# DeltaNet and token mixer on one core: odd head pairs of the last element with their two chunks exchanged

## The chip, the cores and the metric

The kernel runs on one core of a Trainium2 chip. The core has TensorE (PE, the matmuls; its weight loads are listed apart as PEld), VectorE (DVE), ScalarE (ACT), GpSimd (POOL) and SyncE (SP, which here issues every DMA). PE writes its results into PSUM, 8 banks of 2 KB on each of 128 partitions; DVE and ACT read them from there. The time is the device time of one execution in microseconds.

## The reference

Two blocks, one after the other, in float32. The first is DeltaNet over batch 4, 8 heads, 768 tokens, head size 48. Each head keeps a 48x48 state, and each token updates it:

```python
k_n = k / (np.linalg.norm(k, axis=-1, keepdims=True) + 1e-06)
for t in range(S):
    y[:, :, t] = np.einsum('bhd,bhde->bhe', q[:, :, t], state)
    v_old = np.einsum('bhde,bhd->bhe', state, kt)
    state = state + bt[:, :, :, None] * np.einsum('bhd,bhe->bhde', kt, vt - v_old)
```

Its output, seen as 4 x 768 x 384, is the input x of an MLP mixer: `u = x + (relu(x^T w_tok1) w_tok2)^T`, then `u + relu(u w_ch1) w_ch2`, with 256 token features and 1536 channel features.

## The kernel before

**Units and steps.** An element (b, one of the batch of 4) has 768 tokens, cut into 6 units of 128 tokens; units are numbered u = 0 to 23 over the whole batch, so element 3 is units 18 to 23. A unit has two chunks of 64 tokens, cc = 0 and 1. The recurrence goes chunk by chunk, t = 0 to 47, and t = 2u + cc; element 3 is steps 36 to 47.

**Layout.** The 8 heads are four pairs, p = 0 to 3, of two heads, i = 0 and 1. `PAR` names the two halves of the 128 partitions. Data by token (k, v, and what is made from them) are held "stacked": head i of pair p with chunk cc lies on partition half `i ^ cc`, at column slot (p, cc). So one chunk of the two heads of a pair fills both halves. `stacked` (L397) loads k or v so, with 4 DMAs, one per head parity and chunk, each of 4 pairs x 64 tokens. Data by feature (`kqts`, the transposed keys and queries, and the states `s_t`) hold head i on half i, in 48 of its 64 rows (`FEATS`).

**Preparation.** For each unit `load_kq` and `load_v` fetch, and `prep` (L430) computes: ACT squares the stacked keys (`ksq`, L440), DVE and ACT turn the sums into a scale, `cs` multiplies it with beta (L453), from unit 12 on DVE transposes keys and queries (L366, called at L469 and L488), PE multiplies keys with keys and queries (`p_g`, L502), and DVE masks the products into `gm` (L507). `gm` holds per (pair, chunk) three column blocks: `KC` (scaled keys, 48), `TC` (a 64x64 triangular matrix, inverted by DVE in `invert` by rounds of four units, L637 and L642, and joined by PE in `join`), and `GC` (masked query-key products, 64). `load_v` ends with POOL scaling v (L414).

**One step of the recurrence**, `recur(t)` (L740), with the state `s0` and the next state `s1`:

- `p_k` (L757): 8 products, keys times state, weights 48 rows x 64 columns. Head i reads its rows on half i and writes half `i ^ cc`. A 64x64 quarter of the array is given by the row half and the column half of a product; the 8 products of a step use two quarters.
- `rest` (L762), DVE: p_k - v.
- `p_y` (L775), queries times state, and `p_w` (L779), TC times rest, alternating.
- `w_t` (L783), ACT: copy of p_w.
- `p_s` (L791), the state's update, with 64 columns of gm, of which the first 48 are keys, and the second half of p_y (L792), alternating.
- `s1` (L801), DVE: s0 - p_s (a copy at the first step of an element, L803).
- y (L806), ACT: two copies of p_y, one per head parity, 64 partitions x 192 each, into the mixer's input `xb`.

A matmul in float32 shows as two records, so 8 products are 16 records. The first step of an element has no p_k and no first half of p_y; the last has no p_s.

**PSUM.** Four groups of tiles share the 8 banks, one bank each: "prep" 2, "seq" 2, "mlp" 3, and `p_warm` 1, the target of idle matmuls at the start (jobs x, z, Y). p_k, p_y, p_w and p_s each take a free bank of "seq" when they begin and give it back when they have been read.

**The mixer** (`mixer(b)`, L943) follows each element: token products (p_1 L950, p_h L963), transposes (p_ut L973, copied by ACT L977), channel products (p_r L922 by 15 sums of blocks, evacuated by ACT L931, DVE L934 and ACT L938; p_o L1052, added by DVE L981 and L1004). Its products are the bulk of PE's work, and it runs beside the recurrence of the next elements.

**Order.** The planner of the tile library is off. Every job is a Python generator, and the long string `order` (L1124) says which one advances next: `r37*2` advances recur(37) by two yields, `k20` load_kq(20), `p21` prep(21), `m2` mixer(2), `i5` the inversion of round 5, `v18` load_v(18), and so on. Each engine runs its instructions strictly in that order, and SP issues the DMAs in it; the semaphores are put in by the library.

`load_beta` (L238) makes `beta_st`, beta by token and head, with one product per chunk and parity that picks the heads with every second column of the identity (`p_b`, L247).

Of the kernel before, what the change touches and what calls it, by code (L numbers as in the profile page):

```python
# [13 lines left out]
C = 64  # L14
# [9 lines left out]
def kernel(  # L24
# [72 lines left out]

    def ps_seq(shape, name):
        return psum.tile(shape, FP32, name=name, tag="seq", bufs=2)
# [119 lines left out]
    p_warm = psum.tile([128, 4, 128], FP32, name="p_warm", tag="warm", bufs=1)  # L219

    def keep_warm(m):

        zero = warm[:, 0:128]
        while True:
            nc.tensor.matmul(
                p_warm[:, 0:m], zero, zero[:, None, :].to_broadcast([128, m, 128])
            )
            yield

    def warm_tiles():  # L230

        while True:
            for j in range(2):
                for r in PAR:
                    nc.tensor.matmul(p_warm[r, j], warm[r, 0:C], warm[r, 0:128])
            yield

    def load_beta():  # L238
# [6 lines left out]
        for c in range(NQ):  # L245
            for par in range(2):
                nc.tensor.matmul(  # L247
                    p_b[PAR[par ^ c % 2], c], rows[:, c * C : (c + 1) * C],
                    ident[: B * H, par : B * H : 2],
                )  # L250
# [146 lines left out]
    def stacked(dst, src, u):  # L397
        rows = heads_of(src, u)
        for par in range(2):
            for cc in range(2):  # L400
                nc.sync.dma_start(
                    out=dst[PAR[par ^ cc], :, cc], in_=rows[par, cc]
                )
                yield
# [25 lines left out]
    def prep(u):  # L430
# [3 lines left out]
        if u < TU:  # L434
            kp, qp = kpad[slot(u)], qpad[slot(u)]
        gm, kqt, nrm = gm_of(u), kqts[place(u)], nrms[place(u)]
        bet = beta_st[:, b, :, 2 * c : 2 * c + 2]
# [15 lines left out]
        nc.vector.tensor_tensor(  # L453
            out=cs, in0=ksum.rearrange("s (p c) -> s p c", c=2), in1=bet, op=ALU.mult
        )
# [41 lines left out]
        for p in range(NP):  # L497
            for cc in range(2):
                for i in range(2):
                    f = PAR[i] if u < TU else FEATS[i]  # L500
                    nc.tensor.matmul(  # L501
                        p_g[cc][PAR[i ^ cc], p], kqt[f, p, cc, 0], kqt[f, p, cc]  # L502
                    )
        yield
        for cc in range(2):
            assert cc == 0 or before_in(u) is None or before_in(u) in walked
# [233 lines left out]
    def recur(t):  # L740
# [10 lines left out]
        heads = [(p, i, PAR[i ^ cc], PAR[1 - i]) for p in range(NP) for i in range(2)]  # L751

        if c > 0:
            p_k = ps_seq([128, NP, D], "p_k")
            for p, i, r, _ in heads:
                f = FEATS[i]
                nc.tensor.matmul(p_k[r, p], kqt[f, p, cc, 0], s0[f, p])  # L757
# [4 lines left out]
            nc.vector.tensor_tensor(  # L762
                out=rest, in0=p_k, in1=vsts[u][:, :, cc], op=ALU.subtract
            )
            yield
        else:
            rest = vsts[u][:, :, cc]

        assert u in scaled and u in joined
        p_y = ps_seq([128, NP, D], "p_y")  # L770
        p_w = ps_seq([128, NP, D], "p_w")
        for p, i, r, o in heads:
            if c > 0:
                f = FEATS[i]
                nc.tensor.matmul(  # L775
                    p_y[o, p], kqt[f, p, cc, 1], s0[f, p],
                    start=(p == 0), stop=False,
                )
            nc.tensor.matmul(p_w[r, p], gm[r, 2 * p + cc, TC], rest[r, p])  # L779
# [7 lines left out]
        if on:  # L787
            p_s = ps_seq([128, NP, D], "p_s")
        for p, i, r, o in heads:
            if on:  # L790
                nc.tensor.matmul(p_s[PAR[i], p], gm[r, 2 * p + cc, 0:C], w_t[r, p])  # L791
            nc.tensor.matmul(  # L792
                p_y[o, p], gm[r, 2 * p + cc, GC], w_t[r, p],
                start=(c == 0 and p == 0), stop=(p == NP - 1),
            )
        if cc == 1:
            walked.add(u)
        yield
        if on:
            if c > 0:  # L800
                nc.vector.tensor_tensor(out=s1, in0=s0, in1=p_s, op=ALU.subtract)  # L801
            else:
                nc.vector.tensor_copy(out=s1, in_=p_s)  # L803
            yield
        for i in range(2):
            nc.scalar.mul(  # L806
                y[:, :, D * i : D * i + D], p_y[PAR[1 - i]], 1.0 if c else -1.0
# [319 lines left out]
    k4 p1 k5*2 k2*3 p2*2 v0*2 w3*3 p2 k3 p3 p2 p3 p2*4 k5 p2*2 p3 p4 w13 p1 w18 z w2 p0  # L1127
    p3*2 v0 p2 p3 v1 p2*2 p3*3 k5*2 k6 p2 p3 p4 k4 p3*3 p4 w13 w6 p2*2 p1*2 p3*2 k5 p4
    w13 k7*2 p3 i0*6 p5 i0*2 w6 p4*3 k6 p4 i0*4 k6 p4*2 i0*2 k6 i0 p4 w18 k6 z w18*2 i0
    p4*3 p5*2 v1 w13 Y h1*2 h0 i0 k7*2 p6*2 f0*2 w8 w17 f0 h2 h0*2 w8 f1 p5 k7 h0*2 p6  # L1130
    h0*2 h2 p5 v0 w17 f1*2 p7 w8*2 z k8 p4 w6*2 j0 f2 p5*3 k8 w17 f2 j0 h1 v0 j0 h1*3 z
    v1 h1 p7 j0*2 j1 f2 h2*2 w11 h2 z p5 x h2*2 p6 r0*2 p5 w17 r0 k8 w11 v1*2 w11 k8
    w11 r0 p5 p4 k7 w14*2 p5 k9 p5 w14 r0 k8 k9 p5 r1*2 j1 j2 j1 w14 k9*2 h3 f3 r1 p5
    r1 p5 i1 k6 h3 p6*2 Y w9*2 j1 r1 j2 r1 p6 r1 r2 z i1 f3 i1 w0 j1 k9 p8 r2 w0 r2*2
    v2 j2 f3 h3 k9 r2 x h3 p6 h3*2 i1*4 k10 h3 p6 r2*2 w9 p6 i1 r3*2 i1 p7 w0 p6*3 v2*3
    k10*2 w0 k10 p7 r3 v2 w5 r3*4 j3 j2*2 p8 r4*2 j3*2 r4 v3 w9 r4 p7 i1 p7 i1 p8 p7
    w24 i1 p7*2 r4 k8 r4 p8 j3 i1 r5 i1 r5 j3 r4 i1 k10 p7 w5 p7 w5*2 p7 v3 r5*2 p7 p9
    v3*3 w16 r5*3 r6 p6*2 w24 i1 v4 p8*2 v4 p8 w24*2 p6 r6 h5 i1 r6 h5 w27 w16 h4 r6 p7
    h4 p8*2 p6 w16 w27 w16 p7 r6 f4*3 v4 p8*2 r6 w28 p9 p8*2 r7 w27*2 v4*2 h4 p9 r6 p7
    r7 p9 p7 w26 h4*4 p9*3 r7 p9 r7 p9 r7*2 w26*3 p8 w7 p9*4 j4 f5 p8 f5*2 v5 Y p10  # L1140
    w28*2 j4 p10 m0 w7*3 j4*2 r8*2 r7 j4 h5*2 p8*2 h5 p9*4 h5 r8*2 w28 w29 r8 w29 j5
    w29 r8 i2 w15*2 r9 w15 k11 r8 k11 w29 w15 i2*2 v5 h5 j5 i2 m0 r9 i2*4 j5 v5 i2 r9
    i2*3 x j5 r9*3 j5 k11 w22 k11 v7 w22 v7 v5 p10 w4*2 v7 w12 i2 r10 i2*2 w12*2 v5 i2
    w4 m0 i2 r10 p10 w4 i2 m0 k10 k12 w12 r9 k12 v7 w19 i2 r10*5 k12 i2 m0 i2 r11*2 i2
    w19*2 w21 i2 p10 r11 w22 k11 w19 k12 i2 w22 k12*3 v6 w25 v6 r11*2 i2*2 v6 p10 r11
    w31 i2*2 v6 k12*3 v6 p10 i2 p10*2 i2 k12 p10 m0 p10 m0 i2*2 m0 w25 m0 k11 f6 p11*2
    f6*3 m0*2 w21 f7*4 p10 m0*3 f8 w27 p10 w25 m0 w31 k12 p12*2 w31 f8*2 j6 w31 p11 m0
    p11 w23 f8 j6*2 m0 p12 w21*2 w25 j7*3 w29*2 m0 f9*2 w32 p11 r12 j8 p11 p12 w20 p11
    r12 s m0 v7 r12 w25 r12 w23 p10*3 f9 r12 j8 r13 w23 p12 w23 j8 m0 p11 r13*3 p11*2
    w23 x w32 f9 v8 w30 w20 r13*2 k13 w32 w20 p10 r13 p11*3 w20 k13 r14*2 p12 k13 w32  # L1150
    p12 k13*3 m0*2 k13 w30 m0 k13 p11 w30*2 v8 k13 r14 k13*2 r14 p12*2 p11 k13 p12 p13
    r14 p12*3 m0 p12 p13 r14*2 m0 p13 w23 w25 p13 w33 v8*2 m0 j9 r15 p13 m0 w23 p13 r15
    w25 m0 p11 m0 r15 p13 r15 w33 m0*2 r15 p13*2 k14 w33 r15 k14 p13*2 w33 r16 m0 r15
    v8 k14*4 p12 w33 p11 r16 w27 w33 w31 m0 w27 w33 w29 w31*2 p13*2 j9 m0 p13*2 m0 j9
    k14 r16 j9 r16*3 k14 p14*2 r16 m0 r17*2 p14*3 m0*2 r17 i3 r17 i3*4 v10 m0 v10 r17*3
    i3*3 k15 m0 i3*2 v9 r18 i3*2 p14 m0 v10 k14 m0 i3 v9 i3 k15*4 v9 k15*3 m0*2 k14
    i3*9 k14 i3 k14 i3 p14 v9*2 m0*3 k15 r18 k15 p14 i3*6 m0*2 i3 v10 j9 k15 m0*4 k15
    m0*9 r18 p14*2 f11 r18*4 f10*2 p15*2 f12 v10 f12 f11 m0*2 p15*2 f10*2 f13 m0 r19
    p15 f12 f11 m0 f11 m0 r19 p14 f13 j10 f13 m0*2 r19 p15 j10 j11 r19*2 k16*8 m0*2 r19
    j10 j11 v11*3 r20 m0*2 r20 r19 j12 j11 r20 p15 k16 r20 m0 r20*2 p16*2 p15*3 k16 v11  # L1160
    p16*2 r21 r20 r21 m0 p15 r21 p16 r21 j12 p14 j12 k16*2 p14*2 k17*2 r21*3 m0 s k17*5
    p16*2 r22 v11 m0 r22*3 p16 m0 k17*4 r22 s v12 s j13 s p16 r22 k17 p16 r22 r23 p16*3
    v12 r23 v12 p15*4 p17*3 p14 p17 m0 p17 r23 m0 p17*2 r23 m0*2 p16 r23 p17*3 v12 p16
    m0 p17*4 m0 s m0 s*3 p17 m0 f12 m0 j13 s*4 r23 m0*3 v12 m0 i4*5 m0 i4*2 k18*8 m0 i4
    j13 r24 m0 i4 m0*2 r24 f13 r24 k18 m0 i4*2 k18 i4 m0*2 p18 i4 k18 p18*2 m0*2 i4 r24
    i4*3 m0 i4*2 k18 p18 r25 p18 m1 v14 r24 v14*3 i4 r25 m1*2 i4 k19 i4 k19*2 m1*3 r25
    k19 i4*2 v13 j13 r25 i4 p18 r25*2 i4 k19*4 m1 i4*2 m1 r25 v13*2 i4*2 v13 i4 j13 i4
    p19 r26 m1*2 p18 k19*4 m1 v13 r26 p19 m1*5 p18 f14 r26 f14 r26 p18 r26 f15 m1 r26
    m1*3 r26 m1*2 p19 f14 r27*2 f14 m1 r27 f15 p19 f15*2 p19 k20*5 p18 j14 m1*2 p18 p19
    r27*2 j14 j15 m1*2 j14 r27 m1 r27 k20*2 s j15 r28 p18 j15 p19 v14 k20*4 r28 m1*3  # L1170
    k20 m1 v15*2 s*2 p19 v15*2 r28*2 p19 r28 v15 m1 f16*3 r28 r29 p19 p20*2 r28 r29
    p20*2 p19 p20 k21*4 m1*3 p19 k21*4 r29*2 p20 p18*2 p20 m1*3 f17*2 m1*3 r29*3 j16
    m1*2 f17 m1 k21*4 m1*5 r30 j16 m1 r30 p20 m1 p19 m1 p18 m1 j16 p21 r30 p21 p20
    p19*2 p20 r30*3 p20 p21 p20 r31 p20*2 p21 r30 m1 r31*2 v16 r31 v16 m1 p21 f16 k22
# [55 lines left out]
```

## Time and profile before

| what | us |
|---|---|
| median of 3 runs | 647.36 (644.69 to 653.36) |
| the profiled execution | 649.33 |
| its span, first to last instruction | 647.5 |
| PE busy | 609.4 (94%) |
| DVE busy | 445.6 (69%) |
| ACT busy | 258.1 (40%) |
| POOL busy | 107.9 (17%) |
| L757 p_k, one record (mean) | 0.228 |
| L1052 p_o (weights wc, moving r), one record (mean) | 0.330 |
| L934, DVE addition of p_r, one (mean) | 0.684 |

The page of a profile gives busy time by engine, then 40 equal slices of the span with the busy share in tenths and PE's granted clock, the DMA queues, the chain of work that ended last, and groups of instructions by line. Durations of matmul records overlap: a record's duration is its latency, and what a group costs PE is the time from its first start to the next group's first start. A timeline row is start, duration, engine, line, operation, output<-inputs, shapes (output<-input, partitions x elements) and, in brackets, the engine's idle time before it and what ended that. "SPq" rows are DMA issues, and their duration is SP's time to issue them.

### The profile page before, as it was taken

Reading aid. Unit: us, or ns where it says so; the run is one execution under the profiler, and the core shown is the slowest. Engines: PE = TensorE matmul, PEld = TensorE weight load, DVE = VectorE, ACT = ScalarE, POOL = GpSimd, SP = SyncE. Lnnn points to the kernel's source line nnn. Section 1 sums busy time; section 2 is a strip of 40 time slices with the busy share of each in tenths; the row PEclk is TensorE's granted clock in tenths of the full one; section 3 lists DMA queues with packets and bytes.
Section 4 is the critical chain, followed back from the end, with each engine's and each line's share of the span. In section 5 each row is a group of like instructions: output and inputs, shape, how many; then the busy total and the mean of one; then the engine's idle time right before and its main releaser. Section 6 shows DMA issues by size and latency. Waiting matters only on the chain.

```text
span 647.5 us, 22172 instructions
## 1 busy us (share of the span) xinstructions
PE 609.4 (94%) x9486; PEld 529.7 (82%) x9486; DVE 445.6 (69%) x1127; ACT 258.1 (40%) x623; POOL 107.9 (17%) x145
## 2 busy tenths in 40 slices
PE   7568887799999999999999999999999999999997
PEld 5346776567889988967989999869999987999997
DVE  4885664988789848888887989577826353372643
ACT  7748566446541242223633423125324240232240
POOL 1436335234320121002210102000000000000000
PEclk9859778699999999999999999999999999999999
DMA  9847446575643344434445113301110100000000
GB/s 189 176 100 171 105 120 150 115 195 119 138 103 79 88 103 92 97 77 108 96 79 130 45 49 70 75 4 30 28 35 3 31 3 0 25 1 25 1 26 24
DMA packets 135778, 50.30 MB, mean 78 GB/s; under 512 B 114656, under 2 KB 130144, under 8 KB 135680
## 3 DMA queue, kind: packets, MB, share of 16 engines
q1 hardware_dynamic: 135680, 48.89, 33.5%
q8 instruction: 74, 1.21, 0.8%
q14 instruction: 24, 0.20, 0.1%
HBM read 39.42 MB, written 9.44 MB: 75 GB/s over the span
## 4 chain that ended last, share of the span: by engine, by line
PE 83%; DVE 6%; DMA 3%; ACT 2%; issue 2%; SPq 2%; POOL 1%; DVEq 0%; POOLq 0%; ACTq 0%
PE p_o L1052 26%; PE p_r L922 20%; PE p_c L1030 7%; PE p_h L963 5%; PE p L950 5%; PE p_k L757 3%; PE p_y L775 3%; PE p_g L501 3%; PE p_s L791 3%; PE p_z L715 1%; PE p_w L779 1%; DVE sub L637 1%; PE p_y L792 1%; DVE x L642 1%; PE p_ut L973 1%
## 5 line engine op out<-in xcount | busy, mean ns | idle before, releaser
L1052 PE MATMUL p_o<-wc,r 128*128 128x192 f32 x720 | 127.8, 330 | 0.6 <-ACT u_t L977 0.6
L1052 PEld LDWEIGHTS p_o<-wc,r 128*128 128x128 f32 x720 | 116.6, 190 | 3.0 <-ACT u_t L977 1.1
L934 DVE TENSOR_TENSOR r<-r,p_r 128x512 f32<-128x512 f32 x90 | 59.8, 684 | 44.3 <-PE p_r L922 43.3
L981 DVE TENSOR_TENSOR xb<-xb,p_o 128x192 f32<-128x192 f32 x84 | 29.4, 350 | 62.1 <-PE p_o L1052 61.9
L931 ACT COPY r<-p_r 128x512 f32<-128x512 f32 x54 | 31.6, 586 | 99.7 <-PE p_r L922 86.1
L642 DVE TENSOR_TENSOR x<-x,sub 128x84 f32<-128x84 f32 (+24 forms) x178 | 59.2, 333 | 6.1
L637 DVE TENSOR_TENSOR sub<-x 128x84 f32<-128x84 f32 (+24 forms) x178 | 57.4, 322 | 6.3 <-DMA x<-n_dram 2.4
L1030 PE MATMUL p_c<-u_t,wc 128*128 128x256 f32 x216 | 50.8, 386 | 0.6 <-ACT u_t L977 0.6
L414 POOL TENSOR_TENSOR v_st<-v_st,nrm 128x384 f32<-128x384 f32 x24 | 20.7, 865 | 183.2 <-DMA v_st<-in_v_dram 128.5
L1052 PE MATMUL p_o<-wc,s 128*128 128x192 f32 x288 | 50.8, 330 | 0.3 <-DVE xb L981 0.3
L1052 PEld LDWEIGHTS p_o<-wc,s 128*128 128x128 f32 x288 | 46.8, 190 | 1.2 <-DVE xb L981 0.6
L1030 PEld LDWEIGHTS p_c<-u_t,wc 128*128 128x128 f32 x216 | 39.8, 190 | 6.5 <-ACT u_t L977 0.9
L938 ACT ACTIVATE r<-r 128x512 f32<-128x512 f32 x54 | 33.9, 631 | 24.4 <-DVE r L934 24.0
L806 ACT ACTIVATE xb<-p_y 64x192 f32<-64x192 f32 x96 | 31.2, 325 | 24.4 <-PE p_y L792 7.6
L473 POOL TENSOR_TENSOR mb<-mask_c,cs 128x512 f32<-128x512 f32 x20 | 21.0, 1049 | 118.1 <-DVE cs L453 80.3
L922 PE MATMUL p_r<-u_t,wc 128*128 128x128 f32 x288 | 38.5, 277 | 0.0
L783 ACT COPY w_t<-p_w 128x192 f32<-128x192 f32 x48 | 15.3, 318 | 56.9 <-PE p_w L779 56.4
L922 PE MATMUL p_r<-t_d,wc 128*128 128x128 f32 x288 | 37.3, 280 | 0.0
L950 PE MATMUL p<-xb,w 128*128 128x384 f32 x96 | 36.5, 532 | 0.2 <-ACT xb L806 0.2
L922 PEld LDWEIGHTS p_r<-u_t,wc 128*128 128x128 f32 x288 | 35.3, 192 | 0.3
L922 PEld LDWEIGHTS p_r<-t_d,wc 128*128 128x128 f32 x288 | 34.0, 191 | 0.9
L757 PE MATMUL p_k<-s_t,kq 48*64 48x48 f32 x656 | 28.4, 228 | 5.0 <-DVE s_t L801 5.0
(171 smaller groups left out, 1191.7 us busy)
## 6 DMA issues: line engine op xcount, KB each, us to landing
d<-in_moe_w_ch_dram SPq DMA_DIRECT2D x24, 384.0 KB, 4.1
v_st<-in_v_dram SPq DMA_DIRECT2D x96, 48.0 KB, 2.7
out_dram<-xb SPq DMA_DIRECT2D x23, 192.0 KB, 1.9
kst<-in_k_dram SPq DMA_DIRECT2D x64, 48.0 KB, 2.7
n_dram<-gm SPq DMA_DIRECT2D x72, 32.0 KB, 1.9
pads<-in_k_dram SPq DMA_DIRECT2D x24, 96.0 KB, 2.5
pads<-in_q_dram SPq DMA_DIRECT2D x24, 96.0 KB, 2.6
gm<-w_dram SPq DMA_DIRECT2D x72, 32.0 KB, 2.0
```

The source lines that it names most:

```text
L637: nc.vector.tensor_tensor(out=tmp, in0=y[:, :, 0:s, s : s + 1].to_broadcast([n, k, s, w]), in1=y[:, :, s : s + 1, s + 1 : m].to_broadcast( ...
L642: nc.vector.tensor_tensor(out=y[:, :, 0:s, s + 1 : m], in0=y[:, :, 0:s, s + 1 : m], in1=tmp, op=ALU.add,)
L757: nc.tensor.matmul(p_k[r, p], kqt[f, p, cc, 0], s0[f, p])
L806: nc.scalar.mul(y[:, :, D * i : D * i + D], p_y[PAR[1 - i]], 1.0 if c else -1.0)
L922: nc.tensor.matmul(p[:, i], pieces[i // width][:, at : at + 128], f[f"u{n}"], start=first and i == 0, stop=True, skip_group_check=True,)
L931: nc.scalar.copy(o, p)
L934: nc.vector.tensor_tensor(out=o, in0=o, in1=p, op=ALU.add if sign > 0 else ALU.subtract)
L938: nc.scalar.activation(o, o, ACTF.Relu)
L950: nc.tensor.matmul(p_1[dh], piece_of(w1, c, 0)[:, dh * 128 : (dh + 1) * 128], xb[:, c], start=(c == 0), stop=(c == NCH - 1),)
L963: nc.tensor.matmul(p_h, piece_of(w2, j, c * 128)[:, c * 128 : (c + 1) * 128], r1[j], start=(j == 0), stop=(j == NDH - 1),)
L1030: nc.tensor.matmul(p_c[:, k], piece_of(wc1, cb, f * 128)[:, f * 128 : (f + 1) * 128], u_t[:, cb], start=(cb == 0), stop=(cb == NCB - 1),)
L1052: nc.tensor.matmul(p, a[:, m], wc2[:, m, j], start=(start and i == 0), stop=(i == NM - 1), skip_group_check=True,)
```

## The change

It acts on element 3 alone for the layout (units from SW = 18 on, `swaps(u)`), and on all elements for the PSUM tiles.

- In units 18 to 23 the odd pairs (p = 1, 3) exchange their chunks: chunk cc lies in column slot `cc ^ 1`, and so on partition half `i ^ cc ^ 1` (`slot_of`). For one chunk, even and odd pairs now lie on opposite halves, and p_k of a step uses all four quarters.
- `stacked` therefore loads such a unit with 8 DMAs of 2 pairs x 64 tokens instead of 4 of 4 pairs; two are issued per yield.
- `load_beta` picks its columns with a matrix `pick`, built by POOL with four copies at the start. `cs` takes two DVE multiplies instead of one in these units.
- p_k, p_y, p_w, p_s and p_warm are now slices of one tile `p_seq` of three banks. In elements 0 to 2: p_k and p_s share columns 0 to 191 of bank 0, p_w columns 192 to 383 of it, p_y bank 1 at column 0 or 192 by turns, p_warm bank 2. In element 3 even pairs of p_k lie in bank 0 and odd pairs in bank 1, at columns 0 to 95; p_s the same at 96 to 191; p_y of even pairs in bank 1 and of odd pairs in bank 2, at column 192 or 288 by turns; p_w in bank 0 as before.
- In element 3 p_s takes 48 columns of gm (`KC`) instead of 64, the second half of p_y goes ahead of p_s in each pair of products, and one p_w product goes ahead of the first p_y product.
- `order` names the same jobs in the same sequence.

```diff
-    def ps_seq(shape, name):
-        return psum.tile(shape, FP32, name=name, tag="seq", bufs=2)
...
-    p_warm = psum.tile([128, 4, 128], FP32, name="p_warm", tag="warm", bufs=1)
+    SW = 18
+    p_seq = psum.tile([128, 3, 512], FP32, name="p_seq", bufs=1)
+    p_warm = p_seq[:, 2].rearrange("s (m n) -> s m n", m=4)
+
+    def swaps(u):
+        return int(u >= SW)
+
+    def slot_of(u, p, cc):
+        return cc ^ (p & swaps(u))
+
+    ALT = (slice(0, 4, 3), slice(1, 3))
+
+    def halved(t):
+        return t.rearrange("s (x h) d -> s x h d", h=2)
+
+    def in_banks(at, col):
+        return p_seq[:, at : at + 2, col : col + 2 * D].rearrange(
+            "s h (x d) -> s x h d", d=D
+        )
...
+    pick = const.tile([B * H, 2, B * NP], FP32, name="pick")
+    for par in range(2):
+        m = SW // NCH
+        nc.gpsimd.tensor_copy(
+            out=pick[:, par, 0 : m * NP], in_=ident[: B * H, par : m * H : 2]
+        )
+        nc.gpsimd.tensor_copy(
...
-                    ident[: B * H, par : B * H : 2],
+                    pick[:, par],
...
     def stacked(dst, src, u):
         rows = heads_of(src, u)
+        if swaps(u):
+            b, c = divmod(u, NCH)
+            chunks = src[b].rearrange("(x h par) t d -> par h t x d", h=2, par=2)
+            for par in range(2):
+                for e in range(2):
+                    for h in range(2):
+                        at = c * U + (e ^ h) * C
+                        nc.sync.dma_start(
+                            out=dst[PAR[par ^ e], h::2, e],
+                            in_=chunks[par, h, at : at + C],
+                        )
+                    yield
+            return
...
+        if swaps(u):
+            for e in range(2):
+                n = NQ + 1 - 2 * e
+                nc.vector.tensor_tensor(
+                    out=cs[:, :, e].rearrange("s (x h) -> s x h", h=2),
...
+                    e = slot_of(u, p, cc)
                     nc.tensor.matmul(
-                        p_g[cc][PAR[i ^ cc], p], kqt[f, p, cc, 0], kqt[f, p, cc]
+                        p_g[e][PAR[i ^ e], p], kqt[f, p, cc, 0], kqt[f, p, cc]
                     )
...
+        sw = swaps(u)
+        first = [slot_of(u, p, cc) for p in range(NP)]
+        heads = [
+            (p, i, PAR[i ^ first[p]], PAR[1 - i]) for p in range(NP) for i in range(2)
+        ]
+        at = 4 * D + 2 * D * (t % 2) if sw else 4 * D * (t % 2)
+        p_w = p_seq[:, 0, 4 * D : 8 * D].rearrange("s (p d) -> s p d", p=NP)
+        if sw:
+            p_k, p_s, p_y = in_banks(0, 0), in_banks(0, 2 * D), in_banks(1, at)
+            view = halved
+        else:
+            p_k = p_s = p_seq[:, 0, 0 : 4 * D].rearrange("s (p d) -> s p d", p=NP)
+            p_y = p_seq[:, 1, at : at + 4 * D].rearrange("s (p d) -> s p d", p=NP)
...
-                nc.tensor.matmul(p_k[r, p], kqt[f, p, cc, 0], s0[f, p])
+                nc.tensor.matmul(part(p_k, r, p), kqt[f, p, cc, 0], s0[f, p])
...
+            early = sw and (p, i) == (0, 0)
+            if early:
+                w_product()
...
+            def s_product():
+                nc.tensor.matmul(
+                    part(p_s, FEATS[i] if sw else PAR[i], p),
+                    gm[r, g, KC if sw else slice(0, C)], w_t[r, p],
+                    start=not (sw and p % 2), stop=True, skip_group_check=True,
+                )
```

## The prediction

> **What bounds the kernel now.** I read the page's engine sums and slices first, then the chain that ended last, then busy time by stretch.
>
> ```profile
> span 647.5 us, 22172 instructions
> PE 609.4 (94%) x9486; PEld 529.7 (82%) x9486; DVE 445.6 (69%) x1127; ACT 258.1 (40%) x623; POOL 107.9 (17%) x145
> PE   7568887799999999999999999999999999999997
> PEclk9859778699999999999999999999999999999999
> PE 83%; DVE 6%; DMA 3%; ACT 2%; issue 2%; SPq 2%; POOL 1%; DVEq 0%; POOLq 0%; ACTq 0%
> ```
>
> From the ninth slice on (130 us) TensorE is busy in nine tenths or more of every slice, at full granted clock, and 83% of the chain is PE. Element 3's recurrence (steps 36 to 47) runs from 411 to 529 us, inside that stretch. There every microsecond that PE saves or stalls goes straight into the end; the other engines matter only through the moment at which PE must wait for them.
>
> **The gain: four quarters.** The timeline of PE shows one key product and, a little later, one state-and-output product:
>
> ```profile
> 415.50 0.67 PE L757 MATMUL p_k<-s_t,kq 48*64 48x48 f32 x16
> 416.10 6.72 PE L950 MATMUL p<-xb,w 128*128 128x384 f32 x20
> ...
> 424.85 0.25 PE L791 MATMUL p_s<-w_t,gm 64*64 64x48 f32 x1
> ...
> 424.94 0.22 PE L791 MATMUL p_s<-w_t,gm 64*64 64x48 f32 x1
> 425.00 0.22 PE L791 MATMUL p_s<-w_t,gm 64*64 64x48 f32 x1
> 425.06 0.22 PE L791 MATMUL p_s<-w_t,gm 64*64 64x48 f32 x1
> ...
> 425.46 0.21 PE L715 MATMUL p_z<-t,gm 32*32 32x32 f32 x1
> ```
>
> Columns are start and duration in us. The key product's 16 records hold PE from 415.50 to 416.10, 0.60 us: for one chunk all heads use the same two of the four 64x64 quarters. The 32 records of p_s and p_y use all four and take hardly more, 424.85 to 425.46, 0.61 us, in eight rounds of four, 0.057 us apart. Sixteen records on four quarters are four rounds fewer: 0.61 - 4 x 0.057 = 0.38. A saving of 0.22 falls on 11 key products (steps 37 to 47) and on step 47's lone second half of p_y (16 records, 528.79 to 529.39): 12 x 0.22 = **-2.6 us**. Bounds: 0, if two heads on one row half don't overlap, and 12 x 0.30 = 3.6, if the time halves. p_w/p_y and p_s/p_y already fill four quarters, so they stay. The 48 columns of p_s cut a weight load of 135 ns that lies beside the matmuls; I cost it at nothing (if loads set the round, a quarter of 0.057 us in four rounds of 11 steps, 0.6 us).
>
> The Trainium skill, page "TensorE: Matmul & The Clock Gate", section "Part 3: Packing small matmuls", says that a weight load overlaps running matmuls only when its row group differs. By it pairs of heads on the same rows would not overlap, the gain would be 0, and the sum 2.6 us worse. The p_s/p_y rows above contradict it: each round holds two records per row half.
>
> **The price of the fixed banks.** In element 3 p_k and p_s lie in banks 0 and 1, p_y in banks 1 and 2. I assume that the program keeps two engines off one bank at any columns; the trace of before cannot show this, since its tiles each own a bank. Then ACT's two copies of p_y (L806, 0.33 us each) wait for DVE's s1 (L801), and the next p_k waits for those copies. Before, copies and key product often overlap:
>
> ```profile
> 458.44 0.67 PE L757 MATMUL p_k<-s_t,kq 48*64 48x48 f32 x16
> 459.04 2.22 PE L1052 MATMUL p_o<-wc,r 128*128 128x192 f32 x12
> ...
> 458.38 0.63 ACT L938 ACTIVATE r<-r 128x512 f32<-128x512 f32 x1 [0.19 <-DVE r L934]
> 459.03 0.66 ACT L806 ACTIVATE xb<-p_y 64x192 f32<-64x192 f32 x2
> ```
>
> Here the copies of step 41 end at 459.69, behind relus in ACT's order, while p_k of 42 starts at 458.44. With the wait, its second pair (the first in bank 1) starts at 459.8 instead of 458.55: 1.25 us of PE, with the whole mixer queued behind it. I did this for each step from the starts and ends in the timelines: p_k of 44 +0.55 (s1 ends 485.42, copies then to 486.14, p_k began 485.58), of 45 +0.45 (copies end 494.68, p_k 494.24), of 43 +0.15, of 40 and 47 +0.1 each, others 0. In step 38 the copies of 37 stand behind DVE's rest (ends 429.15), so p_y's product starts at 429.95 instead of 429.52: +0.4. Sum **+3.0 us**; bounds 0, if columns alone are ordered, and 5, if each of 11 steps loses 0.2 more.
>
> The Trainium skill, page "PSUM — Partial Sum Buffer", section "PSUM bank collisions raise a hardware error", asks for waits by bank and 32-partition quadrant, not by address. By it the 3.0 stands; were addresses enough, the sum would be 3.0 lower. No run here shows which.
>
> In elements 0 to 2 I find p_k, p_w, p_s in one bank and p_y in another to be the order that two rotating tiles must give anyway (p_y outlives the other three), so I cost the fixed banks there at nothing; if every one of 33 steps lost 0.1 us it would be 3.
>
> **The price of the split loads.** `stacked` issues 8 DMAs for k and for v where it issued 4, in units 18 to 23, all on SP. SP's timeline around unit 21:
>
> ```profile
> 319.58 2.72 SPq L401 DMA_DIRECT2D kst<-in_k_dram  x4
> 322.34 1.10 SPq L584 DMA_DIRECT2D n_dram<-gm  x2
> 323.48 1.44 SPq L609 DMA_DIRECT2D gm<-w_dram  x3
> 325.02 1.82 SPq L357 DMA_DIRECT2D pads<-in_q_dram  x4
> 326.89 4.36 SPq L584 DMA_DIRECT2D n_dram<-gm  x7
> ```
>
> From 304 to 346 us SP issues without a pause (0.04 us between issues), so what is added there delays all that follows. Four issues take 4 x (0.615 + 0.045) = 2.64. A half-size issue over 64 rows is not in the trace: not under 0.43 (L357, 128 pieces on 32 rows), not over 0.615 (L401 itself); I take 0.55, nearer to the same operation. Eight take 8 x 0.595 = 4.76: +2.1 per load, so kst of units 20, 21, 22 end 2.1, 4.2, 6.3 late. Slack is counted at the first reader. ACT squares kst of 21 (L440) at 325.80, landed about 324.0; 4.2 late gives 328.2, and w_t of step 30, next on ACT, ends at 329.1, so p_s moves from 327.60 to 329.2: 1.6. DVE turns q of 21 (second L366, 330.93; landed 329.89); 4.2 late gives 334.1 to 335.2, and p_g moves from 332.12 to 335.3: 3.2 in all. ACT squares kst of 22 at 345.76 (landed 345.60); 6.3 late gives 351.9, w_t of 32 ends 352.9, p_s moves from 348.96 to 353.0: 4.0 in all. Later SP rests (364 to 381 us), and the v loads of 18 to 23 have 4 us or more until use. **+4.0 us**, bounds 0 (drift absorbed) and 5.6 (0.615 per issue: 7.9 late at unit 22).
>
> The rest costs nothing: four small POOL copies for `pick` fall into POOL's idle time from 2.4 to 5.5 us, before p_b at 5.21, which waits for its DMA (if not covered, 0.2 us each); a second small DVE multiply for cs (0.17 us, six units, in DVE's idle time); two-bank reads by DVE and ACT at the same element count.
>
> **Sum.** -2.6 + 3.0 + 4.0 = +4.4 us. The profiled execution took 649.33 us, 1.8 around its span, and would take 653.7; it lies 2.0 above the median shown, 647.36, so against the median I predict **651.8**.
>
> **Rivals.**
> *Net gain, 0.35.* SP's drift is absorbed, or half-size issues cost 0.43 (then +1.2), and the banks cost half: from -2.6 to +1, 644.8 to 648.4. For it: DMA queues are busy under half. Against: SP's unbroken row.
> *Slower by SP, 0.12.* A half-size issue costs the full 0.615, and the drift also reaches DVE's inversion (L637 already waits for x, 343.19) and with it the mixer's additions: 5.6 plus up to 5 for banks, less 2.6, plus 2 on DVE: 655 to 658. It decides from about 0.58 per issue.
> *The change doesn't do what it says, 0.03.* Two heads on one row half don't overlap, because the second's weight load waits for the first's matmul; the key products stay at 0.60, the costs stay too: 647.36 + 7.0 = 654.4.
> *Forecast, 0.48*: 648.5 to 655. Two in a hundred are left for anything else.
>
> Range 644.5 to 658: the ends of the rivals. A measurement of this kernel tells about 2% (13 us) from no change; no case reaches -13 us (0.02 left), and +13 (660.3) only when SP's and the banks' upper ends come together with more drift: 0.06. Within 2%: 0.92.
>
> **What would show it.** Key products of 0.38 us in element 3; p_k of 42 starting only after the copies of 41; kst issues of units 20 to 22 in eights, the last about 6 us later; PE idle before p_s near 328 and 350 and before p_g near 333. If SP's half issues are near 0.43, or p_k starts beside the copies, I am too slow; if p_k stays at 0.60, too fast.

## The result, and the profile after

The changed kernel takes 671.57 us (median of 4 runs, 670.3 to 678.63), the kernel before, run beside it, 648.04 (644.69 to 653.36): a ratio of 1.0378, with a 95% interval of 1.0276 to 1.0479. It is slower by 23.5 us. I had predicted 651.8, within 644.5 to 658: the time lies outside the range. The profiled execution took 671.11 us, again 1.8 around its span.

These are the span, PE's sum, PE's slices with the granted clock, and the engines' shares of the chain, from the page of the kernel after:

```profile
span 669.3 us, 22309 instructions
PE 614.3 (92%) x9486; PEld 530.7 (79%) x9486; DVE 445.1 (66%) x1133; ACT 257.5 (38%) x623; POOL 106.2 (16%) x149
PE   7577788799999999999899899999999999999998
PEclk9969579799999989999889999999999999999999
PE 68%; DVE 10%; DMA 6%; ACT 5%; SPq 5%; issue 4%; POOL 1%; DVEq 0%; ACTq 0%; POOLq 0%
```

PE has the same 9486 records and is busy 4.9 us longer, but its idle time grew from 38.1 to 55.0 us. The chain, which ran over PE for 83%, now runs over it for 68%; DVE, ACT, DMA and SP's issues took the rest. In the second line of digits, the clock is lower than before in the fifth, the sixteenth and the two middle slices.

Next, what PE waited for, over the whole span (releaser, us in total, times, longest), the longest groups of the kernel after. `p_seq` is now the name of every result of the recurrence; L828 is the key product (p_k before), L868 the state's product, L851 the first half of y's product, L894 ACT's copies of y, L887 DVE's s1:

```profile
PE p_seq L828 <- ACT xb L894: 10.1, 15, 1.3
PE p_seq L828 <- DVE s_t L887: 4.5, 3, 3.3
...
PE p_seq L868 <- ACT w_t L860: 3.8, 7, 1.5
PE p_seq L851 <- DVE rest L836: 3.6, 4, 1.9
...
PE p_seq L851 <- ACT xb L894: 1.9, 4, 0.7
```

The same view of the kernel before has one row for p_k, DVE's s1, and none for ACT:

```profile
PE p_k L757 <- DVE s_t L801: 5.0, 4, 3.4
```

Now the key product waits 15 times for ACT's copies of the previous y, 10.1 us.

To see where the time is lost I took the start of ACT's copy w_t, one per step, as a clock along the program, and subtracted the starts of the kernel before. The table gives by how much each kernel falls further behind in three stretches, all from single profiled executions. The experiments, described below, stand beside the changed kernel.

| kernel | steps 0 to 28 | 28 to 36 | 36 to last matmul |
|---|---|---|---|
| after | +11.8 | +8.5 | +0.4 |
| one tile, no exchange | +15.7 | +1.6 | +3.3 |
| one tile, exchange, half-loads on POOL | +13.4 | +1.6 | +0.5 |
| before with split loads | +3.1 | +8.5 | +0.8 |
| one-bank tiles, exchange | +0.5 | +7.5 | +0.4 |
| one-bank tiles, no exchange | +3.2 | 0.0 | 0.0 |
| one-bank tiles, exchange, half-loads on POOL | -1.2 | +0.2 | +0.4 |
| before with 48 columns | -1.8 | +0.2 | 0.0 |

Element 3, the one stretch that my sum worked through, came out at the +0.4 us that the sum gave. The loss lies ahead of it: some 12 us in steps 0 to 28, where I had written zero, and 8.5 in steps 28 to 36, where I had written 4. The first column scatters by some 3 us between kernels that have nothing new there (-1.8 to +3.2), so it is read only where it is far larger. Two kernels are not in the table, the one with ACT as second queue and the one with element 3 in another order: their profiles fell in slow executions, over 1.5% above their fastest, and they are read only for waits, for the clock, and from step 25 on.

PE's idle and busy time tell more. In steps 0 to 28 each kernel issues the same 4622 matmul records. PE's idle time there grows by 7.1 to 8.4 us in the three kernels of one tile (7.4 in the changed kernel, from 15.1 to 22.5) and by -1.0 to +3.2 in the others of the table. The rest of the first column is busy time at a lower granted clock, and from a single profile that can't be put down to the change.

One step in element 2 shows how the first loss arises; PE itself idles only 0.16 us in it, and up to 1.3 in others. From the timelines of ACT and DVE in the kernel before, step 26, start and duration:

```profile
300.25 0.66 ACT L806 ACTIVATE xb<-p_y 64x192 f32<-64x192 f32 x2 [1.00 <-PE p_s L791]
300.21 0.35 DVE L801 TENSOR_TENSOR s_t<-s_t,p_s 128x192 f32<-128x192 f32 x1
```

The two readers run beside each other. The same step in the kernel after:

```profile
312.23 0.35 DVE L887 TENSOR_TENSOR s_t<-s_t,p_seq 128x192 f32<-128x192 f32 x1
...
312.62 0.66 ACT L894 ACTIVATE xb<-p_seq 64x192 f32<-64x192 f32 x2 [1.49 <-DVE s_t L887]
...
313.34 0.67 PE L828 MATMUL p_seq<-s_t,kq 48*64 48x48 f32 x16 [0.16 <-ACT xb L894]
```

DVE reads p_s for s1 until 312.58, and ACT, idle for 1.49 us and with the product complete (its last record starts at 311.87), starts its copies of y 0.04 later. The key product of the next step starts 0.06 after the copies end. Here s1 reads bank 0, the copies read bank 1, and the key product writes bank 0: the copies share a bank with neither. Yet a reader of one bank waits for a reader of another, and a writer for a reader of a bank that it doesn't touch. That happens in every step of the changed kernel that has an s1: no y starts earlier than 0.03 us after its end, where in the kernel before 23 of these 44 y start ahead of it, by up to 2.2 us. The built program says the same. Of its 48 pairs of copies 41 carry a wait for DVE (2 before), and 28 of its 44 key products carry a wait for ACT (6 before):

```
before  L806 Activation xb<-p_y 64x4x48 [waits PE]
after   L894 Activation xb<-p_seq 64x4x48 [waits DVE]
```

My theory from these rows: **A**, the waits are set by tile, and `p_seq` is one tile of three banks, so everything that touches the recurrence's PSUM is put in a row, in all elements. **B**, the rival: the loads and the exchange are the main cause. And beside them, **L**: the loads cost through SP's issue time.

### The profile page after: what moved, and what is told of

The parts are those of the page before. It is cut to its first block, busy times and chain, and to the rows that moved or that the text cites. A ratio compares the mean times of both kernels' runs of the same rounds, so it can differ in the third digit from the quotient of the medians.

```text
span 669.3 us, 22309 instructions
## 1 busy us (share of the span) xinstructions
PE 614.3 (92%) x9486; PEld 530.7 (79%) x9486; DVE 445.1 (66%) x1133; ACT 257.5 (38%) x623; POOL 106.2 (16%) x149
## 4 chain that ended last, share of the span: by engine, by line
PE 68%; DVE 10%; DMA 6%; ACT 5%; SPq 5%; issue 4%; POOL 1%; DVEq 0%; ACTq 0%; POOLq 0%
PE p_o L1140 20%; PE p_r L1010 15%; PE p_c L1118 7%; PE p_h L1051 3%; PE p L1038 3%; PE p_seq L828 3%; SPq L436 3%; ACT xb L894 2%; DVE sub L691 2%; PE p_g L555 2%; PE p_seq L868 2%; PE p_seq L851 2%; DMA kst<-in_k_dram 2%; DVE x L696 2%; PE p_seq L844 2%
## 5 line engine op out<-in xcount | busy, mean ns | idle before, releaser
L894 ACT ACTIVATE xb<-p_seq 64x192 f32<-64x192 f32 x96 | 31.1, 324 | 54.1 <-DVE s_t L887 23.5
L828 PE MATMUL p_seq<-s_t,kq 48*64 48x48 f32 x656 | 25.2, 225 | 12.5 <-ACT xb L894 7.9
L828 PEld LDWEIGHTS p_seq<-s_t,kq 48*64 48x64 f32 x656 | 20.5, 136 | 19.9 <-ACT xb L894 11.6
L860 ACT COPY w_t<-p_seq 128x192 f32<-128x192 f32 x48 | 15.2, 318 | 51.1 <-PE p_seq L844 47.1
```

The costliest lines, as they stand in the source:

```text
L828: nc.tensor.matmul(part(p_k, r, p), kqt[f, p, cc, 0], s0[f, p])
L894: nc.scalar.mul(view(y[:, :, D * i : D * i + D]), p_y[PAR[1 - i]], 1.0 if c else -1.0)
```

## The experiments

### One tile, no exchange

The changed kernel with the exchange switched off; loads and products as before.

```diff
-    SW = 18
+    SW = 24
```

> The changed kernel with the exchange switched off for all elements: loads, products and adds as in the kernel before, but all recurrence results in the one three-bank tile p_seq. Theory A (the waits go by the whole tile, not by its banks: ACT's copies of p_y wait for DVE's s1, and the next p_k for those copies, in every element): the loss of the first 31 steps (18.4 us in the changed kernel's steps, a few of them possibly from the loads) stays, and element 3 waits without the gain: 660 to 668 us, y starts 0.03 us or later after the end of s1 in all steps. Theory B (the loads and the exchange are the cause, the tile costs little): 647 to 651 us.

Measured: 668.56 us against 650.31, ratio 1.0279 (1.0228 to 1.0330). That is 0.6 above A's range. The tile alone costs 18 us; B falls as the main cause. PE waits for ACT's copies before the key product as in the changed kernel:

```profile
PE p_seq L822 <- ACT xb L888: 10.2, 13, 1.4
```

The first stretch grows by 15.7 us, and element 3 by 3.3, without the gain.

### Three tiles of one bank

The same places in the same banks, but each bank a tile of its own. Where the changed kernel reads two banks in one instruction, in element 3, there is one instruction per bank.

```diff
-    p_seq = psum.tile([128, 3, 512], FP32, name="p_seq", bufs=1)
+    p_seq = [psum.tile([128, 512], FP32, name=n, bufs=1) for n in ("p_seqa", "p_seqb", "p_seqc")]
...
-            nc.vector.tensor_tensor(out=view(rest), in0=p_k, in1=vs, op=ALU.subtract)
+                for h in range(2):
+                    nc.vector.tensor_tensor(
+                        out=rest[:, h::2], in0=p_k[h], in1=vsts[u][:, h::2, cc ^ h],
+                        op=ALU.subtract,
+                    )
```

> The changed kernel with p_seq cut into three tiles of one bank; in element 3 the reads that spanned two banks become one instruction per bank (rest and s1 twice, y four times in place of twice). Theory A: the waits of elements 0 to 2 go (some 15 to 18 us); left are the gain of 2.6, the loads' price of 4 to 6, and 0 to 2 for 12 x 4 to 6 more small instructions: 648 to 655 us, and y starts beside or ahead of s1 again in elements 0 to 2. Theory B (loads and exchange): 665 us or more, since nothing of them is touched.

Measured: 658.85 us, ratio 1.0117 (1.0062 to 1.0172), 3.9 above the upper end of what A expected and below B's. The first stretch is back at +0.5 us. What is left lies in steps 28 to 36, +7.5 us, more than the 4 to 6 that I had allowed for the loads.

And without the exchange:

> The three one-bank tiles, and the exchange switched off for all elements: the kernel before, but for fixed banks in place of two rotating ones. Theory A: fixed places cost nothing where each bank is a tile of its own: 645 to 649 us. A rival within A (fixed places themselves cost, because p_y of the next step always finds the same bank and waits for ACT): 650 to 655 us. Theory B: 645 to 649 us as well.

Measured: 653.33 us, ratio 1.0045 (1.0011 to 1.0079): in microseconds inside what the second form gave, but the kernel before itself stood at 650.31 in these runs, and against it the price is 2.9. This kernel and the one-tile kernel differ only in how PSUM is cut into tiles, and stand at 1.0045 and 1.0279 of the kernel before: the waits by tile are shown as the cause of some 15 us. Step 26 again, from the timeline of the kernel with one-bank tiles and no exchange:

```profile
303.32 0.66 ACT L905 ACTIVATE xb<-p_seqb 64x192 f32<-64x192 f32 x2 [1.01 <-PE p_seqa L865]
303.34 0.35 DVE L893 TENSOR_TENSOR s_t<-s_t,p_seqa 128x192 f32<-128x192 f32 x1
```

The two readers now start together, 0.02 us apart, when the product is done. Whether these 2.9 us are a price of fixed places stays open: the profile loses 3.2 us in steps 0 to 28, no more than the split-load kernel, which has the old rotating tiles, and another kernel with the same tiles (below) stands at 1.0003.

### The loads alone

The kernel before, with the k and v loads of units 18 to 23 in eight issues, the data in its old places.

```diff
     def stacked(dst, src, u):
         rows = heads_of(src, u)
+        if u >= 18:
+            for par in range(2):
+                for cc in range(2):
+                    for h in range(2):
+                        nc.sync.dma_start(
+                            out=dst[PAR[par ^ cc], h::2, cc],
+                            in_=rows[par, cc, :, h::2],
+                        )
+                    yield
+            return
```

> The kernel before, with the k and v loads of units 18 to 23 in 8 half-size issues, the data in its old places. The price of the loads alone. By the prediction's term +4.0 us (bounds 0 and 5.6); with the 0.605 us that one half-size issue took in the changed kernel, eight take 5.2 in place of 2.6, so the k loads of units 20, 21, 22 come 2.5, 5.1, 7.7 us later: +4 to +6, 651 to 654 us. Theory B (the loads are the main cause): +12 us or more, above 659 us. If SP's delay is hidden: 647 to 649 us.

Measured: 662.56 us, ratio 1.0177 (1.0139 to 1.0215), +11.5 us by the ratio. Taken alone that is B's case, not mine: nearly three times the +4.0. B still isn't the main cause, since the one-tile kernel has 18 us without split loads; there are two causes, and A had been too narrow. The trace places 8.5 us of this kernel's loss in steps 28 to 36 and 0.8 in element 3 (the v loads); another 3.1 stand in the first stretch, where it is the kernel before up to the loads of units 18 and 19 (from 268 us). The path of PE's longest wait in steps 28 to 36, in three views of this kernel (its timeline, of SP, of ACT and of PE):

```profile
311.11 4.97 SPq L403 DMA_DIRECT2D kst<-in_k_dram  x6
316.18 0.54 SPq L594 DMA_DIRECT2D n_dram<-gm  x1
316.76 1.25 SPq L403 DMA_DIRECT2D kst<-in_k_dram  x2
...
320.86 0.52 ACT L450 ACTIVATE ksq<-kst 128x384 f32<-128x384 f32 x1 [5.00 <-DMA kst<-in_k_dram]
321.40 0.66 ACT L816 ACTIVATE xb<-p_y 64x192 f32<-64x192 f32 x2
...
322.12 0.31 PE L785 MATMUL p_y<-s_t,kq 48*64 48x48 f32 x2 [2.53 <-ACT xb L816]
```

SP needs 311.11 to 318.01 for the eight issues of unit 20's k. ACT stands 5.00 us before its square of that k; behind it in ACT's order are the copies of y, and PE waits 2.53 us for the copies before it may write the next p_y. One half-size issue takes 0.605 us (median of the 48 for k, least 0.596), nearly as long as a whole one (0.615). The wait is not all of the loss: of the 8.5 us in steps 28 to 36, 6.2 are idle time of PE and 2.2 are longer busy time: from 324.17 to 327.58, starting 2.1 us after this wait, PE's granted clock was 0.50.

### The half-loads on another queue

One-bank tiles with the exchange; the second of each two half-loads is issued by POOL, or by ACT.

```diff
-                        nc.sync.dma_start(
+                        (nc.sync, nc.gpsimd)[h].dma_start(
```

> The three one-bank tiles with the exchange, and the second of each two half-size loads of units 18 to 23 issued by POOL in place of SP: SP has four issues per load again. Theory L (the loads cost through SP's issue time, 0.605 us for each half-size issue, in the stretch where SP issues without a pause): the 7.6 us that the one-bank kernel lost between steps 28 and 33 go, and the time is 646 to 651 us. Rival (the cost is in the transfers, twice as many of half the size): 655 to 659 us as with the one-bank tiles. Second rival (POOL issues in its own order, behind products of v that wait for other loads): some k loads come later than on SP, 655 us or more, with POOL's waits in front of the issues.

Measured with POOL: 648.18 us against 649.94, ratio 1.0003 (0.9962 to 1.0044). The transfers are the same in number and size, so the rival that blamed them falls, and with the time the second rival, POOL's own order; the loss of steps 28 to 36 goes from 7.5 to 0.2 us. SP and POOL around unit 21's k:

```profile
318.45 3.16 SPq L437 DMA_DIRECT2D kst<-in_k_dram  x4
...
316.83 2.38 POOL L437 DMA_DIRECT2D kst<-in_k_dram  x4
```

The eight issues are spread over two engines, and POOL has its 2.4 us to spare.

> The same with ACT as the second queue. Theory L: SP's delay goes, but ACT spends up to 0.6 us in each of the 4 added issues per load, 2.4 us for each of the k loads of units 20 to 22 between its copies of w_t and y: 647 to 655 us. Rival (transfers): 655 to 659 us. If an issue on ACT holds it for the time that SP needs and stands ahead of w_t at each step: above 659 us.

Measured with ACT: 662.48 us, ratio 1.0211 (1.0156 to 1.0266): the last of the three cases. ACT's issues hold ACT, and PE waits behind it. ACT's timeline in that kernel:

```profile
296.32 3.20 ACTq L437 DMA_DIRECT2D kst<-in_k_dram  x4
299.57 0.87 ACT L1063 ACTIVATE r<-p 128x384 f32<-128x384 f32 x2 [2.93 <-DMA kst<-in_k_dram]
```

and a row of what PE waited for:

```profile
PE p_h L1068 <- ACT r L1063: 2.6, 1, 2.6
```

The four issues stand between w_t and a relu; the relu's idle time, put down to a DMA in the row, is the 3.20 us of issuing, and p_h waits 2.6 for the relu. Around this wait PE's granted clock was 0.50 for 6.83 us (from 298.87), and step 26 alone fell 5.4 us further behind the kernel before; from step 25 to 47 this profile loses 11.8. An engine that PE waits for is no place for DMA issues, however idle its sum (40%). The Trainium skill's page "Perfetto Trace Analysis", section "DMA Optimizations", says that splitting a DMA may let the whole finish sooner where the DMA engines are idle, and that spreading DMAs over the sync, scalar and GpSimd engines may help where the generation of descriptors is the bottleneck. Here the split is what made SP late, moving half of the issues to POOL took the loss back, and moving them to ACT did not.

### Both causes, one removed

The changed kernel, its one tile kept, with only the half-loads moved to POOL.

> The changed kernel as it is, one tile of three banks, with only the second of each two half-size loads of units 18 to 23 issued by POOL. If the two costs add (tile-wide waits some 13 to 16 us in elements 0 to 2, loads some 8 us), the loads' share goes and the waits stay: 661 to 666 us, ratio 1.018 to 1.026. Rival (the loads hide behind the waits or the other way round, since both delay the same steps): less than 4 us better than the changed kernel, 667 us or more.

Measured: 665.70 us against 651.99, ratio 1.0235 (1.0186 to 1.0285), against 1.0378 for the changed kernel. The ratios differ by 1.4%, about 9 us, and the trace has +1.6 us in steps 28 to 36 in place of +8.5: the loads' share goes and the tile's stays, so the two costs add. By time the sum is rough: the tile alone (18 us) and the loads alone (11.5) make 29.5 us, where the changed kernel lost 23.5, with an interval from 18 to 31.

### The 48 columns alone

The kernel before with 48 columns for p_s in every step but the first of each element; p_k, p_w and p_s share one of the two rotating tiles.

```diff
-                nc.tensor.matmul(p_s[PAR[i], p], gm[r, 2 * p + cc, 0:C], w_t[r, p])
+                rows, cols = (FEATS[i], KC) if c > 0 else (PAR[i], slice(0, C))
+                nc.tensor.matmul(p_s[rows, p], gm[r, 2 * p + cc, cols], w_t[r, p])
```

> The kernel before with one part of the change alone: the state's product p_s takes 48 columns in place of 64 in all elements (but for the first step of each), without the exchange and with unsplit loads; p_k, p_w and p_s share one of the two rotating tiles. In the changed kernel the 32 records of p_s and p_y took 0.558 us in place of 0.611 in element 3. Theory C (the 48-column weight load sets the round): 0.053 us in each of some 40 steps, -2.1 us, ratio 0.995 to 0.999, the phase at 0.558 in all elements. Rival (the 0.053 came from the exchange's other order of quarters): the phase stays at 0.611, ratio 1.000.

Measured: 648.92 us against 649.94, ratio 1.0016 (0.9979 to 1.0053). In element 3 the 32 records of p_s and p_y take 0.611 to 0.613 us in each of the ten steps whose records are all in the trace, so theory C falls. The 0.558 us of the changed kernel's element 3 comes with the exchange (its quarters, or p_y ahead of p_s; the two were not told apart).

### Element 3 in another order

One-bank tiles, the exchange, half-loads on POOL, and the order changed in element 3 alone: y of step 41 after rest of step 42, y of step 43 after the key product of step 44, and the shared bank first in s1 and in the copies of y.

```diff
-v22 m2*6 r41*2 m2*4 v21 m2*5 r41 m2 r42*2 j22
+v22 m2*6 r41*2 m2*4 v21 m2*6 r42*2 r41 j22
...
-m2*11 r43 m2*3 r43*3 j23*2 r44 m2*3
+m2*11 r43 m2*3 r43*2 j23*2 r44 r43 m2*3
```

> One-bank tiles, the exchange, the second half-loads on POOL, and in element 3 the waits of p_k for y taken apart by order: y of step 41 after the key product and rest of step 42, y of step 43 after the key product of step 44, s1 and the copies of y on the shared bank first. In the kernel without this, the steps of element 3 lose 3.6 us at p_k and gain 3.2 by shorter phases. Theory (those waits are only order): 1.25 at step 42 and 0.6 at step 44 go, and 0.1 to 0.3 at each of steps 38, 40, 43 and 45; from step 36 to the end -1.5 to -2.5 us against the kernel before, time 645 to 648 us, ratio 0.994 to 1.000. Rival (the copies, put later, hold up the next p_y or rest instead): element 3 stays at +0.4 or more.

Measured: 649.90 us against 651.99, ratio 0.9975 (0.9934 to 1.0015). From step 36 to the last matmul its trace gains 1.15 us against the kernel before, where the same kernel without this lost 0.4; the step into 42 goes from +0.98 to -0.26, into 44 from +0.39 to -0.13, and the key product's wait for y is gone from PE's waits in this stretch. In the kernel without the new order, the row for steps 36 to 47 read:

```profile
PE p_seqb L825 <- ACT xb L906: 1.5, 3, 0.9
```

The gain is short of the 1.5 to 2.5 expected. At steps 38, 40 and 45, where 0.1 to 0.3 us each were to go, the steps got longer instead: 0.49, 0.18 and 0.46 us are added there, 0.23, 0.10 and 0.23 without the new order. In these steps the rival, copies that are put later hold up others, has its part; which of the edits did it was not told apart. As a time it can't be told from the kernel before.

## Why the prediction was wrong

**Elements 0 to 2, "I cost the fixed banks there at nothing".** This is the step that failed first, and the larger part of the miss. I assumed that the program keeps two engines off one *bank*, found p_k, p_w, p_s in one bank and p_y in another, and saw no new conflict. The waits go by the *tile*, and the change had put three banks into one. My bound, 3 us if each of 33 steps lost 0.1, was a bound on the wrong mechanism; in the trace the stretch to step 28 lost 11.8, 13.4 and 15.7 us in three kernels with the one tile, and -1.8 to +3.2 in the table's kernels without. In the changed kernel 9.4 us of PE's waits there are for ACT's copies (7.5 before key products, 1.9 before y's first half), a kind that the kernel before doesn't have in this stretch; PE's idle time grew by 7.4, since some earlier waits went. The section that I cited, "PSUM bank collisions raise a hardware error" of the Trainium skill's page "PSUM — Partial Sum Buffer", asks for waits by bank and quadrant; the program that was built has more than that, and the runs show its price, not whether fewer waits would be safe within one bank. None of my rivals held this case. The profile's own group rows could not have shown it either; the diff could, since it replaces tiles of one bank by one of three.

**The loads, +4.0 (bounds 0 and 5.6).** Late loads that make PE wait are what the runs show, but the term was too small by a factor of two: 7.5 to 8.5 us in steps 28 to 36. The drift was mis-sized first. A half-size issue, taken at 0.55 us between 0.43 and 0.615, measured 0.605, so the rival "slower by SP" was past its point of 0.58. The k load of unit 21, predicted at 4.76 us, took from 334.90 to 341.05 in the kernel after:

```profile
334.90 6.15 SPq L436 DMA_DIRECT2D kst<-in_k_dram  x8
```

Seven of these eight issues took 0.60 to 0.62 us and one 1.59; single long issues stand in the kernel before too (1.72 in unit 19's k). The stalls that I priced were three, all from units 21 and 22. Unit 20's k was to be 2.1 us late and harmless. It landed at 320.75 in the kernel with split loads, with step 28 4.6 us behind, against 310.98 in the kernel before: 5.1 us late (4.1 in the changed kernel). At 2.1 the copies of y behind ACT's square of that k would still have ended, by an estimate from its rows, ahead of the next p_y of the kernel before, which started at 314.87; at 5.1 they cost PE 2.53 us. In the changed kernel the same late load (ACT idle for 3.98 us before that square) came out 1.9 us long at y's first half: the copies of y ended at 329.29, DVE's rest, which by the tile waits for them, started at 329.33, and PE at 329.74.

The sum also had no term for what follows a wait. The same 1567 matmul records in steps 28 to 36 kept PE busy for 99.9 us at a mean granted clock of 1.00 in the kernel before, 103.3 at 0.97 in the changed kernel, 102.1 at 0.98 with split loads and 104.5 at 0.95 with one-bank tiles and the exchange. So 2.2 to 4.5 us of this loss are longer busy time at a lower clock, and 3.0 to 6.2 are idle time; with the half-loads on POOL both are gone (100.1 at 1.00). The rival gave 655 to 658 by taking 5.6 for this term, still too low.

**The gain of four quarters, -2.6: right, and a little small.** The key product of step 39, from the PE timeline of the kernel after:

```profile
457.99 0.45 PE L828 MATMUL p_seq<-s_t,kq 48*64 48x48 f32 x16
458.37 0.87 PE L1061 MATMUL p_ut<-ident,xb 128*128 128x128 f32 x6
```

From 457.99 to 458.37 it holds PE for 0.38 us, the predicted 0.38; the median over the 11 steps is 0.379 (0.598 before), and step 47's lone half of y's product takes 0.378. The rule of "Part 3: Packing small matmuls" (the Trainium skill, page "TensorE: Matmul & The Clock Gate"), by which the gain would have been 0, is contradicted here a second time; the rival "doesn't do what it says" falls with it. The state's product gave 0.053 us in each of 11 steps (0.611 to 0.558), which I had mentioned as 0.6 us "if loads set the round" and left out; the reason was wrong, since 48 columns alone left the 0.611 as it was. In sum 12 x 0.22 + 11 x 0.053 = 3.2 us.

**The banks in element 3, +3.0: right.** Each step of element 3 should gain 0.27 us; what it falls short of that is the stall. So read, the changed kernel stalled 1.29 us at step 42 (predicted 1.25), 0.59 at 44 (0.55), 0.53 at 45 (0.45), 0.46 at 38 (0.4), 0.35 at 43 (0.15), 0.23 at 40 and 0.22 at 47 (0.1 each), 3.6 us over all steps. The largest, with ACT's relu ahead of the copies as I had read it in the kernel before (ACT and PE timelines of the kernel after):

```profile
478.91 0.63 ACT L1026 ACTIVATE r<-r 128x512 f32<-128x512 f32 x1 [0.19 <-DVE r L1022]
479.55 0.66 ACT L894 ACTIVATE xb<-p_seq 64x192 f32<-64x192 f32 x2
...
480.26 0.45 PE L828 MATMUL p_seq<-s_t,kq 48*64 48x48 f32 x16 [1.22 <-ACT xb L894]
```

The kernel with one-bank tiles has the same 3.6 us of stalls in element 3, where p_k and p_y share the middle bank: cutting the tile by banks doesn't remove this part, as predicted. Since each bank is then a tile of its own, no run tells a wait by bank from one by tile here. Gain 3.2 and stalls 3.6 leave the +0.4 us of the table; both terms came out 0.6 larger than predicted, and that their sum still fits is luck.

**The sum.** -2.6 + 3.0 + 4.0 = +4.4 us was predicted. The trace gives 0.4 for element 3, 8.5 for the loads, 11.8 for elements 0 to 2 up to step 28 and 1.1 ahead of the first step (-1.3 to +1.5 in the table's other kernels): 21.8 us, the span's growth from 647.5 to 669.3. I spent the work on the element that the change names, and a whole-kernel edit in its first lines got one sentence.

**The edits costed at nothing.** No run shows a cost of `pick`, of the second multiply for cs or of the 48 columns; none of them was removed alone except the last.

## What to carry to other kernels

Look at what an edit does to the units in which dependencies are kept before looking at banks or addresses: a tile that grows over several buffers makes readers of different buffers wait for each other, everywhere it is used, and that shows as an engine idle with its input complete and released by an engine that only reads. A queue that issues without a pause is a bound like an engine: twice the issues cost twice the time even if the bytes stay, the whole drift reaches the first consumer whose engine has something urgent behind it, and the cure is an engine that nobody waits for. A wait may cost more than its length: with each of the four longest of PE in the busy stretch, 1.9 to 2.6 us, its clock was at half for 3.4 us or more. When a gain is spread over one stage and an edit over all, cost the edit first.

## What the runs showed of the hardware

- SP's time to issue a DMA did not go by its bytes or pieces: 64 rows of four 192-byte pieces took 0.615 us, 64 rows of two 0.605, and 32 rows of four pieces of 640 or 768 bytes 0.43. The half-load of 64 rows took 0.595 us on POOL and 0.624 on ACT (medians of the issues for k).
- A wait of PE can cost more than its length. From 145 us on, the traces of the eleven kernels have four idle gaps of PE of 1.9 to 2.6 us, and with each of them comes a stretch at a granted clock of 0.50: 3.41 us after 1.90 in the changed kernel, 3.41 after 2.53 with split loads, 10.24 after 2.61 with one-bank tiles and the exchange, 6.83 around 2.63 with ACT as second queue. None of the 14 gaps of 1.0 to 1.8 us has one. Three more such stretches, of 3.41 us, follow two gaps of 0.5 to 0.8 us within 2 us of each other. In the kernel before, there is none from 140 to 640 us.
- Ahead of 140 us the clock was at 0.50 for 51 us in the kernel before, and for 38 to 51 in the table's other kernels without the one tile; for 51 to 68 in the three with it; and for 72 in the two profiles that are not in the table, both with one-bank tiles. One profile each can't tell how much of that is the tile's. Over all executions run beside each other, the mean granted clock was 0.938 to 0.954 in the kernel with one tile and no exchange, 0.946 to 0.966 in the same kernel with one-bank tiles.
